# Attention, GLU and MLP on one core: decode order of the first group, the place of the short block's split, one decode pace, and the order of output steps in two MLP pairs

## The chip, the core and the metric

The kernel runs on one NeuronCore of a Trainium2 chip. TensorE (PE) multiplies; VectorE (DVE), ScalarE (ACT) and GpSimd (POOL) do the element work; SyncE (SP) issues the transfers. The metric is the device time of one execution in microseconds (us); lower is better.

## The reference

Three stages run one after the other on 2304 tokens of width 512.

```python
# 1: linear attention with random features, per batch and head
h = x @ omega.T - sum(x*x)/2;  phi = exp(h - max(h)) / sqrt(m)
num = phi(q) @ (phi(k).T @ v);  x = num / (phi(q) @ sum(phi(k)) + 1e-6)
# 2: RMS norm and gated unit (d_ff 1536)
xn = x / rms(x) * rms_g
x = (silu(xn @ w_gate) * (xn @ w_val)) @ w_out
# 3: MLP (d_ff 2048)
out = silu(x @ w_in) @ w2_out
```

The weights arrive in 64-bit floating point, as two 32-bit words for each number.

## The kernel before, in words

**Numbers.** Each operand of the large products is held as a high and a low half (`hi`, `lo`), and a product is three matmuls (high by high, high by low, low by high), listed in `PASS`. Tokens stand in five blocks: four of 512 and one of 256, the short block (`j` = 4). The hidden width is cut into columns of 128, numbered `f`.

**Weights.** A weight is loaded by SP into one of two raw buffers, decoded by five DVE operations (L146 to L157) and two POOL additions (L160) into an f32 tile `m`, and then split: ACT copies the high half into a slot (L412), DVE subtracts for the low half (L416). Gate and value weights are also scaled on ACT (L168).

**Units.** After the attention and the first three columns of the gated unit comes a list `groups`: units u = 0 to 8 are the gated unit's columns 3 to 11, one column each with three weights (gate `g`, value `v`, output `o`); u = 9 to 16 are pairs of MLP columns, with four weights each (two `i`, two `p`). `std` is 9: u = 9 and 10 are computed in the plain way, the others by `quad`, which works on blocks 0 and 1 together with seven half products in place of eight, and needs sums of the token blocks (`token_sums`) and of the weights (`sum12`, `sum34`). The token sums are made twice: before u = 0, and during u = 9 and 10. The second time they are five DVE additions, two to four POOL subtractions and splits of 128x1024.

**Order on each engine.** Every engine runs its instructions in the order in which the program emits them. The program emits PE work in steps, and each step tells its length; the main loop adds it to `due`. When `due` exceeds `wq.pace`, the next job of the weight queue is emitted (`tick`) and the pace is taken off. A job that needs a slot waits until one is free. While `wq.hold` is true no job is taken in this way. `need` emits jobs at once until the weight that is asked for exists. The pace is 1.6 for u = 5 to 8 (`A_PACE`) and 2.0 for the other units (`M_PACE`); before u = 0 it is 1.6.

**Output steps.** The products with `w_out` are cut into steps (`g2_glu`, L259: three matmuls and one DVE addition into `ya`, L270; in the last gated unit also an ACT copy, L272, and a DVE subtraction, L249, which give the MLP its input). They are handed on as the list `pend` and emitted between the projections of the next unit. In a plain pair `g1_mlp` emits a whole projection of 12 matmuls (L205) and then a number of them. The result of a projection is split by ACT and DVE (L198, L199) before its output step can start. PSUM has four banks for projections and four for output steps; an output step takes a bank again when the DVE addition of the fourth step before it has read it.

**First group.** The last token sum of blocks before u = 0 calls `end(1)`, which loads the value weight into the raw buffer that this sum has used; the gate's load goes out earlier, with `end(0)`. Then the queue's first jobs are an empty one, the decode of the value weight, the decode of the gate.

**Short block.** `glu_block` ends with the product of gate and value of the short block on DVE (L621) and its split (L198 on ACT, L199 on DVE). Behind it ACT has the first bank copies of the next `quad` (L529), on which the third of its half products waits.

Of the kernel before, what the change touches and what calls it, by code (L numbers as in the profile page):

```python
# [20 lines left out]
def kernel(  # L21
# [14 lines left out]
    nc = tc.nc  # L36
# [62 lines left out]
    def ps_tile(which, shape):  # L99
        p, tag, n = pools[which]  # L100
        return p.tile(shape, F32, tag=tag, name=tag, bufs=n)
# [88 lines left out]

    PASS = [(0, 0), (0, 1), (1, 0)]
    HALVES = [slice(0, 64), slice(64, P)]
    M_PACE, A_PACE, T_PACE = 2.0, 1.6, 1.2
    W_EARLY, GRAIN, GATE = 3, 3, 3

    def split_h(s, j):
# [110 lines left out]
            yield 0.216 * nn  # L307

    KH = KC // 2
    tok, sums, ready = {}, [], set()  # L310
    NSTD = 2
    std = next(u for u, g in enumerate(groups) if g[0] == 2)

# [54 lines left out]
    class WeightQueue:  # L368
# [28 lines left out]
        def plan(self, u):  # L397
            kind, _ = groups[u]
            (a0, a1), bs = self.keys(u)
            st = self.st  # L400
            ss = State()
            ss.t = {}
            hw = KH * P
            mf = lambda key: st[key].m.bitcast(F32)

            def dec(key, n):
                for k in range(7):
                    w_decode((0, 0, key, None), st[key], k, n)

            def split_hi(x, tl):  # L410
                v = tl.rearrange("p (a n) -> p a n", a=2)
                nc.scalar.activation(out=v[:, 0, :], in_=x, func=AF.Copy)  # L412
                return v

            def split_lo(x, v, eng=nc.vector):
                eng.tensor_tensor(out=v[:, 1, :], in0=x, in1=v[:, 0, :].bitcast(F32), op=ALU.subtract)  # L416

            def hi(key):
                if key[1] in "gv":
                    w_scale(st[key])  # L420
                st[key].t = split_hi(mf(key), self.slot(key))

            def lo(key):
                split_lo(mf(key), st[key].t)
                wt[key] = st[key].t

            def sum12():
                ss.x = pools["w"][1].tile([P, KC * P], F32, tag="ws", name="ws", bufs=1)
                m0, m1 = mf(a0), mf(a1)
                less(ss.x[:, :hw], m1[:, :hw], m1[:, hw:], ALU.add)  # L430
                less(ss.x[:, hw:], ss.x[:, :hw], m0[:, :hw])

            def sum34():
                m0, m1 = mf(a0), mf(a1)
                less(m1[:, :hw], m0[:, :hw], m1[:, :hw])
                less(m1[:, hw:], m0[:, hw:], ss.x[:, hw:])

            def shi(n):
                ss.t[n] = split_hi(ss.x if n == 0 else mf(a1), self.slot(("s", u, n)))

            def slo(n):
                split_lo(ss.x if n == 0 else mf(a1), ss.t[n], nc.vector if kind == 2 else nc.gpsimd)
                wt["s", u, n] = ss.t[n]

            load = self.load
            if kind == 1:
                jobs = [
                    *[(0,)] * (u == 0),
                    (0, lambda: dec(a1, 1), lambda: load(u + 1, 1, 1)),
                    *self.tail,  # L450
                    (0, lambda: dec(a0, 0), lambda: load(u, bs[0], 0)),
                    (1, lambda: hi(a1)),
                    (0, lambda: lo(a1)),
                    (1, lambda: hi(a0)),
                    (0, lambda: lo(a0), sum12),
                    (0, sum34),
                    (1, lambda: shi(0)),
                    (0, lambda: slo(0), lambda: dec(bs[0], 0), lambda: load(u + 1, 0, 0)),
                    (1, lambda: shi(1)),
                    (0, lambda: slo(1)),  # L460
                ]
                self.tail = [(1, lambda: hi(bs[0])), (0, lambda: lo(bs[0]))]
            elif std <= u < std + NSTD:
                jobs = [
                    (0, lambda: dec(a1, 1), lambda: load(u, bs[1], 1)),
                    *self.tail,
                    (0, lambda: dec(a0, 0), lambda: load(u, bs[0], 0)),
                    (1, lambda: hi(a1)),
                    (0, lambda: lo(a1)),
                    (0, lambda: dec(bs[1], 1), lambda: load(u + 1, 1, 1)),  # L470
                    (1, lambda: hi(a0)),
                    (0, lambda: lo(a0)),
                    (0, lambda: dec(bs[0], 0), lambda: load(u + 1, 0, 0)),
                    (1, lambda: hi(bs[1])),
                    (0, lambda: lo(bs[1])),
                    (0,),
                    (1, lambda: hi(bs[0])),
                    (0, lambda: lo(bs[0])),
                ]
                self.tail = []  # L480
            else:
                jobs = [
                    (0, lambda: dec(a0, 0)),
                    (0, lambda: dec(a1, 1), lambda: load(u, bs[0], 0)),
                    (1, lambda: hi(a0), lambda: load(u, bs[1], 1)),
                    (1, lambda: lo(a0), lambda: hi(a1)),
                    (0, lambda: lo(a1), sum12),
                    (0, sum34),
                    (1, lambda: shi(0)),
                    (0, lambda: slo(0)),  # L490
                    (1, lambda: shi(1), lambda: dec(bs[0], 0)),
                    (0, lambda: slo(1), lambda: load(u + 1, 0, 0)),
                    (1, lambda: hi(bs[0]), lambda: dec(bs[1], 1)),
                    (0, lambda: lo(bs[0]), lambda: load(u + 1, 1, 1)),
                    (1, lambda: hi(bs[1])),
                    (0, lambda: lo(bs[1])),
                ]
            self.jobs += [(n, fns) for n, *fns in jobs]
# [25 lines left out]
    def quad(u, ys, hs):  # L524
# [9 lines left out]
        def more(n=1):  # L534
            return [v for v in [next(ys, None) for _ in range(n)] if v is not None]
# [23 lines left out]
        yield step  # L559
        product(w1, 0, half(0, 0), pa, True)  # L560
        copy(pb, pa)
        yield from more()
        wq.need(("s", u, 0))
        s12 = wt["s", u, 0]
# [46 lines left out]
    def glu_block(f, j, hs, ys, n):  # L611
        full = blocks[j] == TB * P
        cuts = [(0, 6), (6, 12)] if full else [(0, 12)]
        for nm in "gv":
            w = wt[1, nm, f]
            p = ps_tile("ps_g" if full else "ps_y", [P, blocks[j]])
            for n0, n1 in cuts:
                yield (n1 - n0) * blocks[j] / 2365
                part(w, j, p, n0, n1)
                if nm == "v" and n1 == 12:  # L620
                    nc.vector.tensor_tensor(out=s, in0=s, in1=p, op=ALU.mult)  # L621
                elif n1 == 12:
                    s = pools["s"][0].tile([P, blocks[j]], F32, tag="s", name="s", bufs=pools["s"][1])
                    nc.scalar.activation(out=s, in_=p, func=AF.Silu)
                for _ in range(n[nm]):
                    c = next(ys, None)
                    if c is not None:
                        yield c
        hs[f] = split_h(s, j)

    def take(ys, n):
        for _ in range(n):
            c = next(ys, None)
            if c is not None:
                yield c
# [5 lines left out]
    def stream():  # L641
# [25 lines left out]
        for u, (kind, fs) in enumerate(groups):  # L667
            first, last = kind == 2 and fs[0] == 0, u == len(groups) - 1
            done = u + 1 == std
            wq.pace = A_PACE if std - 4 <= u < std else M_PACE  # L670
            hs = {j: {} for j in range(NB)}
            if std <= u < std + NSTD:
                out_of = lambda j: g2_mlp(fs, j, hs[j], first, False, False)
                ys = iter(pend)
                wq.hold = first
                yield from g1_mlp(fs[0], 0, hs[0], (), take(ys, 4))
                yield from g1_mlp(fs[1], 0, hs[0], (), take(ys, 4))
                yield from g1_mlp(fs[0], 1, hs[1], (), ys)
                wq.release(*wq.keys(u - 1)[1])
                yield from g1_mlp(fs[1], 1, hs[1], (), out_of(0))  # L680
                wq.hold = False
                if first:
                    now, later = token_sums(
                        lambda k: w_tile(1, 7, F32) if k == 2 else wq.slot(("t", k), F32),
                        lambda n: wq.release(("t", 1 - n)),
                    )
                    sums.extend(now)
                if u == std + NSTD - 1:
                    sums.extend(later)
                yield from g1_mlp(fs[0], 2, hs[2], (), out_of(1))  # L690
                yield from g1_mlp(fs[1], 2, hs[2], (), ())
            else:
                yield from quad(u, iter(pend), hs)
# [840 lines left out]
```

## Time and profile before

| | |
|---|---|
| median of 3 runs | 975.37 us (974.75 to 975.85) |
| the profiled execution | 974.8 us |
| its span, first to last instruction | 972.9 us |
| mean granted TensorE clock | 0.995 |
| PE busy | 949.4 us, 98% of the span |
| DVE busy | 698.6 us, 72% |
| ACT, POOL busy | 431.5 us, 416.7 us |

1.9 us lie outside the span. Times within the trace count from its start. In a row of the timeline stand the start, the length from the first start to the last end of the merged instructions, the engine, the line, the operation, what it writes and reads, the shape and the count; in brackets the idle time of the engine just before and what ended it. The end of a matmul is modelled, so distances are taken from start to start.

### The profile page before, as it was taken

How to read it: one execution, taken by the hardware profiler on the slowest of the kernel's cores; microseconds unless marked ns; L12 is line 12 of the kernel's file. 1: busy time of each engine (PE TensorE's matmuls, PEld its weight loads, DVE VectorE, ACT ScalarE, POOL GpSimd, SP SyncE). 2: the span in 40 equal slices, each digit the busy share in tenths (PEclk: the TensorE clock that was granted, in tenths of full speed). 3: DMA queues.
4: the chain of work that ended last, by engine and by line, in shares of the span. 5: the costliest groups of instructions: out<-in, count | busy, mean ns of one | idle time of the engine just before them, and what ended most of it. 6: DMA issues, size and time to landing. Idle time of an engine off the chain costs nothing. (4 is left out here: it accounts for less than half of the span.)

```text
span 972.9 us, 17023 instructions
## 1 busy us (share of the span) xinstructions
PE 949.4 (98%) x6570; PEld 793.6 (82%) x6570; DVE 698.6 (72%) x1368; ACT 431.5 (44%) x978; POOL 416.7 (43%) x402
## 2 busy tenths in 40 slices
PE   8999999997999999999999989999999999999998
PEld 6888878886888888887887867887888888888887
DVE  6998989646677677777779796467675666666643
ACT  6999786533324324323332335534333333333321
POOL 8888745305445335336436231442333343424200
PEclk9999999998999999999999999999999999999999
DMA  8655543011111111111122120011011111111023
GB/s 192 167 135 132 144 126 96 1 44 44 47 62 44 44 44 44 44 44 43 44 65 66 44 66 1 22 44 44 25 63 35 53 44 43 44 44 44 1 76 120
DMA packets 79490, 60.42 MB, mean 62 GB/s; under 512 B 27313, under 2 KB 73649, under 8 KB 79409
## 3 DMA queue, kind: packets, MB, share of 16 engines
q1 hardware_dynamic: 79136, 59.26, 21.3%
q8 instruction: 52, 0.85, 0.4%
q14 instruction: 30, 0.24, 0.1%
q10 hardware_dynamic: 272, 0.07, 0.0%
HBM read 49.87 MB, written 4.72 MB: 56 GB/s over the span
## 5 line engine op out<-in xcount | busy, mean ns | idle before, releaser
L160 POOL TENSOR_TENSOR m<-m,raw 128x512 int32<-128x512 int32 x136 | 208.2, 1533 | 332.4 <-DVE m L157 169.4
L205 PE MATMUL g<-xs,w 128*128 128x512 f32 x1056 | 255.5, 390 | 0.0
L205 PEld LDWEIGHTS g<-xs,w 128*128 128x128 f32 x1056 | 197.7, 188 | 40.8
L292 PE MATMUL y<-w,h 128*128 128x512 f32 (+1 forms) x870 | 206.6, 388 | 1.5 <-DVE h L199 1.3
L292 PEld LDWEIGHTS y<-w,h 128*128 128x128 f32 x870 | 162.3, 188 | 35.8 <-DVE h L199 1.8
L259 PE MATMUL y<-h,w 128*128 128x512 f32 (+1 forms) x648 | 159.4, 373 | 9.6 <-ACT h L198 5.7
L199 DVE TENSOR_TENSOR h<-s,h 128x512 fp32r<-128x512 f32 (+1 forms) x134 | 101.1, 760 | 74.9 <-ACT h L198 74.1
L259 PEld LDWEIGHTS y<-h,w 128*128 128x128 f32 x648 | 114.8, 191 | 33.0 <-ACT h L198 6.1
L270 DVE TENSOR_TENSOR ya<-y,ya 128x512 f32<-128x512 f32 (+1 forms) x200 | 123.4, 632 | 25.5 <-PE y L259 25.4
L303 DVE TENSOR_TENSOR ya<-y,ya 128x512 f32<-128x512 f32 (+1 forms) x127 | 84.8, 681 | 62.9 <-PE y L292 62.3
L198 ACT ACTIVATE h<-s 128x512 fp32r<-128x512 f32 (+1 forms) x134 | 77.0, 585 | 118.6 <-DVE s L621 60.7
L518 PE MATMUL g<-xs,w 128*128 128x512 f32 x360 | 91.7, 390 | 0.0
L412 ACT ACTIVATE w<-m 128x512 fp32r<-128x512 f32 x74 | 46.6, 629 | 90.7 <-POOL m L160 67.9
L416 DVE TENSOR_TENSOR w<-m,w 128x512 fp32r<-128x512 f32 x65 | 60.4, 930 | 29.6 <-ACT w L412 29.3
L1051 ACT ACTIVATE e<-b,nb 128x128 f32<-128x128 f32 x272 | 75.9, 424 | 7.7 <-issue 4.3
L518 PEld LDWEIGHTS g<-xs,w 128*128 128x128 f32 x360 | 67.1, 188 | 13.9
L518 PE MATMUL g<-w,w 128*128 128x512 f32 x270 | 69.1, 391 | 1.9 <-ACT g L529 1.9
L205 PEld LDWEIGHTS y<-xs,w 128*128 128x128 f32 x480 | 61.7, 191 | 5.3 <-DVE ya L270 3.1
L205 PE MATMUL y<-xs,w 128*128 128x256 f32 x480 | 62.6, 283 | 2.7 <-DVE ya L270 2.7
L518 PEld LDWEIGHTS g<-w,w 128*128 128x128 f32 x270 | 49.9, 188 | 12.8 <-ACT g L529 2.8
L1019 DVE TENSOR_REDUCE small<-b 128x4 f32<-128x512 f32 (+1 forms) x80 | 51.3, 642 | 6.3 <-PE b L1002 2.9
L541 ACT ACTIVATE s<-s 128x512 f32<-128x512 f32 x21 | 13.3, 632 | 77.7 <-DVE s L546 77.7
(119 smaller groups left out, 1159.6 us busy)
## 6 DMA issues: line engine op xcount, KB each, us to landing
raw<-in_moe_w_out_dram SPq DMA_DIRECT2D x28, 512.0 KB, 3.6
raw<-in_moe_w_in_dram SPq DMA_DIRECT2D x16, 512.0 KB, 3.6
raw<-in_moe_w_gate_dram SPq DMA_DIRECT2D x12, 512.0 KB, 3.6
raw<-in_moe_w_val_dram SPq DMA_DIRECT2D x12, 512.0 KB, 3.6
qT<-e SPq DMA_DIRECT2D x72, 64.0 KB, 2.6
x<-in_k_dram SPq DMA_DIRECT2D x16, 256.0 KB, 3.8
x<-in_q_dram SPq DMA_DIRECT2D x16, 256.0 KB, 3.4
va<-in_v_dram SPq DMA_DIRECT2D x32, 128.0 KB, 4.2
```

The source lines that it names most:

```text
L160: tt(out=mi, in0=mi, in1=(low if step == 5 else high).bitcast(I32), op=ALU.add)
L198: nc.scalar.activation(out=ht[:, 0, :], in_=s, func=AF.Copy)
L199: nc.vector.tensor_tensor(out=ht[:, 1, :], in0=s, in1=ht[:, 0, :].bitcast(F32), op=ALU.subtract)
L205: nc.tensor.matmul(out=ps, lhsT=w[:, a, cc * P:(cc + 1) * P], rhs=xs[j][:, c, cc, :], start=(n == 0), stop=(n == 3 * KC - 1),)
L259: nc.tensor.matmul(out=ps, lhsT=wt[1, "o", f][:, a, d * P:(d + 1) * P], rhs=hs[f][:, c, :], start=(n == 0), stop=(n == nn - 1),)
L270: nc.vector.tensor_tensor(out=y[:, d, :], in0=ps, in1=y[:, d, :], op=ALU.add)
L292: nc.tensor.matmul(out=ps, lhsT=hs[f][:, a, t * P:(t + 1) * P], rhs=wt[2, "p", f][:, c, d0:d1], start=(n == 0), stop=(n == nn - 1),)
L303: nc.vector.tensor_tensor(out=o[:, t, d0:d1], in0=ps, in1=o[:, t, d0:d1], op=ALU.add)
L416: eng.tensor_tensor(out=v[:, 1, :], in0=x, in1=v[:, 0, :].bitcast(F32), op=ALU.subtract)
L518: nc.tensor.matmul(out=ps, lhsT=w[:, a, (c0 + c) * P:(c0 + c + 1) * P], rhs=x(b, c), start=(start and n == 0), stop=(n == 3 * KH - 1), ski ...
L1019: nc.vector.tensor_reduce(out=st.mx.rearrange("p (j e) -> p e j", e=2)[:, e], in_=st.ps[e], axis=AX.X, op=ALU.max)
L1051: nc.scalar.activation(out=st.e[r][:, :, h, :] if blocks4 else st.e[r][:, h, :], in_=src.rearrange("p (a f) -> p a f", a=4) if blocks4 els ...
```

## The change

In `plan`, the first group (u = 0) has a job list of its own: the gate is decoded first, then comes the empty job, then the value weight, and the splits follow in the same order. The raw buffers are refilled in that order too. The pace is 1.8 for all units below `std`, and before them. At the end of the jobs of u = 9 a job stands that can't be taken (it asks for 1024 free slots); the program takes it off after the fourth projection of this pair, so no job of u = 10 is emitted before that. The split of the short block goes into a list `wait`, which `quad` empties after its first bank copy, or a plain pair at its start. In the two plain pairs the first four projections are cut into two halves, with output steps after each half: in u = 9 two and one for each projection (before, they stood as four, four and four behind the first three), in u = 10 two and two, then one and one, and at the fourth projection all that is left, with the steps of block 0.

```diff
-    M_PACE, A_PACE, T_PACE = 2.0, 1.6, 1.2
+    M_PACE, A_PACE, T_PACE = 2.0, 1.8, 1.2
...
-            if kind == 1:
+            if u == 0:
                 jobs = [
-                    *[(0,)] * (u == 0),
+                    (0, lambda: dec(a0, 0), lambda: load(u, bs[0], 0)),
+                    (0,),
+                    (0, lambda: dec(a1, 1), lambda: load(u + 1, 1, 1)),
+                    (1, lambda: hi(a0)),
+                    (0, lambda: lo(a0)),
+                    (1, lambda: hi(a1)),
+                    (0, lambda: lo(a1), sum12),
+                    (0, sum34),
+                    (1, lambda: shi(0)),
+                    (0, lambda: slo(0), lambda: dec(bs[0], 0), lambda: load(u + 1, 0, 0)),
+                    (1, lambda: shi(1)),
+                    (0, lambda: slo(1)),
+                ]
+                self.tail = [(1, lambda: hi(bs[0])), (0, lambda: lo(bs[0]))]
+            elif kind == 1:
+                jobs = [
                     (0, lambda: dec(a1, 1), lambda: load(u + 1, 1, 1)),
                     *self.tail,
                     (0, lambda: dec(a0, 0), lambda: load(u, bs[0], 0)),
...
                 self.tail = []
+                if u == std:
+                    jobs.append((1 << 10,))
...
         copy(pb, pa)
+        while wait:
+            wait.pop(0)()
         yield from more()
...
+        if full:
+            hs[f] = split_h(s, j)
+        else:
+            wait.append(lambda: hs.update({f: split_h(s, j)}))
+
+    def mlp_block(f, j, hs, ys, n):
+        wq.need((2, "i", f))
+        p = ps_tile("ps_g", [P, blocks[j]])
+        for k in range(2):
+            yield 3 * KH * blocks[j] / 2365
+            part(wt[2, "i", f], j, p, 3 * KH * k, 3 * KH * (k + 1))
+            yield from take(ys, n[k])
+        s = pools["s"][0].tile([P, blocks[j]], F32, tag="s", name="s", bufs=pools["s"][1])
+        nc.scalar.activation(out=s, in_=p, func=AF.Silu)
         hs[f] = split_h(s, j)
...
-            wq.pace = A_PACE if std - 4 <= u < std else M_PACE
+            wq.pace = A_PACE if u < std else M_PACE
...
-                yield from g1_mlp(fs[0], 0, hs[0], (), take(ys, 4))
-                yield from g1_mlp(fs[1], 0, hs[0], (), take(ys, 4))
-                yield from g1_mlp(fs[0], 1, hs[1], (), ys)
-                wq.release(*wq.keys(u - 1)[1])
-                yield from g1_mlp(fs[1], 1, hs[1], (), out_of(0))
+                while wait:
+                    wait.pop(0)()
+                each = [(2, 1)] * 4 if first else [(2, 2), (1, 1), (0, 0), (0, 0)]
+                for n, k in enumerate(each):
+                    if n == 3:
+                        ys = chain_of(ys, out_of(0))
+                        wq.release(*wq.keys(u - 1)[1])
+                    yield from mlp_block(fs[n % 2], n // 2, hs[n // 2], ys, k if n < 3 else (k[0], 9))
                 wq.hold = False
                 if first:
+                    assert wq.jobs.pop(0)[0] == 1 << 10
```

## Rows read from the trace of the kernel before

**Rows 1.** The page: its first line.
```profile
span 972.9 us, 17023 instructions
```

**Rows 2.** Windows: length, busy us (instructions) of PE, PEld, DVE, ACT, POOL; clock, DMA.
```profile
220.00:230.00 10.00, 5.30 (x12) 3.90 (x13) 7.34 (x11) 4.71 (x12) 7.95 (x8) 0.68 0.35 106
460.00:470.00 10.00, 8.63 (x38) 7.14 (x39) 8.33 (x18) 4.41 (x10) 3.82 (x3) 1.00 0.35 107
560.00:570.00 10.00, 6.58 (x34) 5.46 (x33) 10.00 (x13) 2.89 (x5) 5.33 (x4) 0.92 0.33 99
```

**Rows 3.** Timeline, PE in the third gated unit: the pace of matmuls without waits.
```profile
308.94 1.58 PE L205 MATMUL y<-xs,w 128*128 128x256 f32 x12
310.35 0.86 PE L259 MATMUL y<-h,w 128*128 128x512 f32 x3
...
313.16 1.53 PE L518 MATMUL g<-xs,w 128*128 128x512 f32 x6
314.53 0.84 PE L259 MATMUL y<-h,w 128*128 128x512 f32 x3
```

**Rows 4.** Timeline of the last steps before u = 0, all engines.
```profile
203.20 0.38 SPq L136 DMA_DIRECT2D raw<-in_moe_w_gate_dram  x1
...
212.88 1.22 DVE L331 TENSOR_TENSOR xs<-raw,xs 128x1024 fp32r<-128x1024 f32 x1
...
213.44 5.60 PE L205 MATMUL g<-xs,w 128*128 128x512 f32 x24
...
217.55 0.43 DVE L146 TENSOR_SCALAR m<-raw 128x512 uint32<-128x512 uint32 x1 [2.85 <-DMA raw<-in_moe_w_val_dram]
...
219.23 0.69 DVE L270 TENSOR_TENSOR ya<-y,ya 128x512 f32<-128x512 f32 x1
219.40 2.69 POOL L160 TENSOR_TENSOR m<-m,raw 128x512 int32<-128x512 int32 x2 [18.58 <-DVE m L157]
...
220.88 1.50 DVE L149 TENSOR_SCALAR raw<-raw 128x512 uint32<-128x512 uint32 x1
...
223.31 0.68 DVE L228 TENSOR_TENSOR s<-s,g 128x512 f32<-128x512 f32 x1
...
224.70 5.79 PE L259 MATMUL y<-h,w 128*128 128x512 f32 x12 [5.66 <-ACT h L198]
...
230.28 5.74 PE L205 MATMUL g<-xs,w 128*128 128x512 f32 x24
```

**Rows 5.** Waits of PE: engine, line, releaser; us in total, times, longest.
```profile
PE y L259 <- DVE ya L270: 3.3, 4, 1.3
...
PE g L518 <- ACT g L529: 1.9, 2, 1.4
```

**Rows 6.** Timeline, ACT at the start of the quad of u = 6.
```profile
460.42 0.42 ACT L198 ACTIVATE h<-s 128x256 fp32r<-128x256 f32 x1 [5.07 <-DVE s L621]
```

**Rows 7.** Timeline from the last gated unit to block 0's output in u = 9.
```profile
557.60 0.42 DVE L146 TENSOR_SCALAR m<-raw 128x512 uint32<-128x512 uint32 x1
...
562.50 1.58 PE L205 MATMUL y<-xs,w 128*128 128x256 f32 x12
...
564.66 3.14 DVE L249 TENSOR_TENSOR xs<-ya,xs 128x512 fp32r<-128x512 f32 x2
...
568.46 2.93 PE L205 MATMUL y<-xs,w 128*128 128x256 f32 x12 [2.71 <-DVE ya L270]
...
570.72 0.42 DVE L146 TENSOR_SCALAR m<-raw 128x512 uint32<-128x512 uint32 x1
...
593.83 5.69 PE L292 MATMUL y<-w,h 128*128 128x512 f32 x24 [0.18 <-DVE ya L270]
```

**Rows 8.** One window, from block 2 of u = 9 to u = 10; columns as in group 2.
```profile
599.35:623.94 24.59, 24.59 (x121) 20.85 (x120) 12.17 (x15) 12.64 (x22) 10.98 (x5) 1.00 0.07 22
```

**Rows 9.** Timeline, plain pairs: two splits, and PE's wait for one.
```profile
609.50 2.92 DVE L199 TENSOR_TENSOR h<-s,h 128x512 fp32r<-128x512 f32 x2 [1.77 <-ACT h L198]
...
664.69 3.47 PE L292 MATMUL y<-w,h 128*128 128x512 f32 x14 [1.32 <-DVE h L199]
```

More of the change, by code (lines that the diff above doesn't have):

```diff
@@ L309 @@
     KH = KC // 2
-    tok, sums, ready = {}, [], set()
+    tok, sums, ready, wait = {}, [], set(), []
     NSTD = 2
```

## The prediction

> **What bounds the kernel now.** I read the page first, then PE's clock and load in windows of 10 us, then the list of PE's waits, and last the timeline of all engines around each place where PE waits. PE bounds the kernel: its matmuls fill nearly the whole span [rows 1], and where nothing holds it back a matmul of 512 columns follows the one before it after (314.53 - 313.16)/6 = 0.228 us, one of 256 columns after (310.35 - 308.94)/12 = 0.1175 us [rows 3]. So the change can only win back time in which PE stands still or runs at the lower clock. There is little of it and it lies in a few places, so I price place by place: matmuls counted in the code between two rows, times these two durations, against the distance of the rows.
>
> Before u = 0: 213.44 to 230.28 holds 24 + 12 = 36 matmuls of 512, 8.2 us of work in 16.84 us; lost 8.6 [rows 4]. 5.66 of this is one wait. After it the granted clock is at the lower of its two levels, 1.2 GHz, for most of the window (mean 0.68) [rows 2], and 12 matmuls take 230.28 - 224.70 = 5.58 where 2.74 would do: 2.84 more [rows 4].
>
> At the starts of quads: two waits for a bank copy (L529), 1.9 together [rows 5].
>
> At the end of u = 7: of the four waits of an output step for a `ya` addition the longest, 1.3 [rows 5]; the other three lie in the next place.
>
> From the short block of u = 8 to block 0's output in u = 9: 562.50 to 593.83 is 31.33 us and holds 78 matmuls of 512 and 36 of 256, 17.8 + 4.2 = 22.0 us; lost 9.3 [rows 7]. A part is clock: the window of 560 shows 0.92 [rows 2].
>
> In u = 10: one wait of 1.3 for a split [rows 9].
>
> Together 22.4 us, out of 974.8 us for the profiled execution. All steps below are sums against this 974.8; the median of the runs shown, 975.37, is 0.6 above it.
>
> **The first group's order.** Here the chain is: the value weight's raw buffer comes free with the last token sum (L331, 212.88 + 1.22), its load lands at 217.55, DVE stands before its decode for 2.85 us, then decodes it, adds a `ya`, and decodes the gate as well; only then comes the product of gate and value of block 0 (L228, 223.31) [rows 4]. PE's output steps wait for the split of this product. The gate's words were loaded at 203.20, so its decode needs no transfer. With the change it starts where L331 ends, about 214.1; five operations last 219.23 - 217.55 = 1.68, so it ends about 215.8, its two POOL additions (2.69) about 218.6, and the two `ya` additions fit before 217.55. The value's decode then starts between 217.55, if POOL does not hold it up, and 218.6, if it does; L149 beside a POOL addition took 1.50 where L146 took 0.43 [rows 4], so I take 218.6. Then L228 starts at 218.6 + 1.68 = 220.3 and not at 223.31: 3.0 won (4.1 at the other end). PE's wait shrinks from 5.66 to about 2.6 (1.6). The same number of jobs, transfers and splits is issued; the refill of the value's raw buffer, for u = 1, moves one job back, a whole unit ahead of its use. If the clock stays up after the shorter wait, 2.84 are won too, less about 0.5 for the second output matmul, which still waits for the low half: 2.3. Sum 5.3.
>
> **The short block's split.** The bank copies of the quad stand behind L198 on ACT, which waited 5.07 us for the DVE product L621 [rows 6]. With the change the first copy needs only its own matmuls. What is late next is the copy `e`, which now stands behind the split and is read three half products later, and the split itself, read by the last four output steps of the quad. I take the whole 1.9; the other end is 0, if PE then meets `ya` additions that are just as late.
>
> **The even pace.** In `glu_block` a half projection and an output step add 1.30 + 0.65 = 1.95 to `due`. A pace of 1.6 leaves 0.35 over each time, so that from u = 5 a second job falls into the same step every fifth time or so; 1.8 leaves 0.15, and in u = 0 to 4, where 2.0 took less than one job for each step, it is just above one. The weight decodes are not fewer, but in u = 7 the output weight's decode and the POOL split behind it come one or two steps (1.3 to 2.0 us) earlier, and the MLP decodes behind them are no longer pushed together. I take 1.0 of the 1.3 (ends 0 and 1.3). What u = 0 to 4 pay is put at nothing: no wait of [rows 5] lies there, and DVE has room; if that cover is gone, a wait as in u = 7 is the price, 1.3.
>
> **The stop in the queue and the spread steps.** By 557.60 all four weights of u = 9 have been decoded; the decodes from 557.60 to 570.72 are three (557.60, 561.27, 570.72), all for u = 10 [rows 7]. They fall where DVE has two operations for each output step, because the last unit also splits `xs`; two of these subtractions took 3.14 beside POOL's additions, and PE then waited 2.71 [rows 7]. With the stop these three decodes leave the stretch: 3 x 1.68 on DVE, 3 x 2.69 on POOL [rows 4], and two low splits of 0.69. Then the first projections of u = 9: with four steps behind a projection DVE needs 4 x 2 x 0.69 + 0.69 = 6.2 us while PE needs 24 x 0.228 = 5.5; with three steps it is 4.8 against 21 x 0.228 = 4.8. So DVE no longer falls behind, but gains nothing either: the short block's product and split, which now stand there, are not hidden, about 0.8 (two operations of 256 columns, ACT's took 0.42 [rows 6]), and I leave one more wait of 0.5. Won 8.0 of 9.3. The low end is the stall in front of 568.46 alone: 568.46 - 562.50 less 12 x 0.1175 and 3 x 0.228, 3.9. The cut of a projection in two halves itself costs nothing, since the number of matmuls and of loads of weights stays.
>
> **What the moved decodes cost.** The three decodes now come behind the fourth projection of u = 9, beside the second token sums. There DVE and POOL are busy 12.17 and 10.98 of 24.59 us, and PE waits nowhere [rows 8]. The decodes add 3 x (1.68 + 2.69) + 1.4 = 14.5, so 37.6 us of DVE and POOL work, of which most reads SBUF on both engines, stand against 24.59. They can run side by side only in part: two splits took 2.92 instead of 1.4 [rows 9]. I expect that splits come late twice in the plain pairs, at 1.3 each, the wait at 664.69 being the nearest row: 2.6 lost. Ends: 0, and 8 (the rival below). The wait at 664.69 itself I leave as it is.
>
> **Sum.** 5.3 + 1.9 + 1.0 + 8.0 - 2.6 = 13.6; 974.8 - 13.6 = 961.2, and 961.8 with the 0.6 of the median.
>
> **Rivals.** (1) The clock falls again at the shortened wait before u = 0. A wait of 2.71 was followed by a lower clock, the window that holds one of 1.4 shows 1.00 [rows 2, 5, 7]; 2.6 lies by the first, but the stretch in front of the 2.71 was itself broken by waits, and here PE works without a gap before. Price 2.3: 964.1.
>
> (2) The moved decodes and the token sums shut each other out. If no DVE and POOL operation overlaps there, 13 us of the 37.6 do not fit into the stretch, and late splits are passed on into u = 10, where PE waits more often; I put 8 in place of 2.6, that is six waits of 1.3: 967.2. For it speaks L149's 1.50, against it that the list of waits shows PE almost never waiting for a split. The Trainium skill, in "SBUF — State Buffer", section "Who interferes with whom", says that DVE operations with two SBUF inputs, or in the modes that use both ports, and GpSimd operations that read SBUF exclude one another for a whole instruction. By that rule this rival's count is the right one and the sum would be 967.2; L149's 1.50 agrees with it.
>
> (3) The even pace doesn't help: the backlog on DVE before u = 9 comes from the `xs` splits alone. Then the pace gives 0 and only 3.9 of 9.3 come back: 1.0 + 4.1 more, 966.9. Against it: the decodes stand in the very rows of the stall.
>
> (4) Slower: the two input weights of u = 10 are not ready when it starts. Between the stop and 623.94 lie 24.59 us, in which steps for about eleven jobs are emitted; the low split of the second weight is the seventh. It decides when fewer than seven are taken; then `need` emits them in line, each 1.68 + 2.69 + 2 x 0.69 = 5.8 us of waiting, with 2.84 for the clock as behind 5.66. Two of these are 17.2 against 13.6 + 2.6 = 16.2 won elsewhere: 1.0 over the time before, 976.4.
>
> (5) The change doesn't do what it says: the waits pass to the next late operation, and the time stays at 975.
>
> **Chances.** The forecast 0.42, the clock 0.30, the crowded pair 0.14, no help from the pace 0.08, slower 0.03, no change 0.03. A difference of 0.2% is about what a measurement of this kernel can tell from none. Faster by more: 0.94; within: 0.03; slower: 0.03. The range reaches down to 957.5 (all of 9.3, the other end of the decode's start) and up to 967.5, which takes in cases 1 to 3.
>
> **What would show it.** Right: before u = 0 DVE writes the gate's decode behind L331 with no wait for a transfer, and PE's wait there is 1.6 to 2.7 with the clock above 0.9 in that window; no wait of L518 for L529; three decodes fewer between the last gated unit's second block and u = 9; fewer than 2 us lost over the 78 and 36 matmuls; new waits for L199 or `h` between block 2 of u = 9 and the end of u = 10, of 1 to 3 us. Wrong: PE's wait before u = 0 over 4 us, a clock near 0.7 there, or waits for splits in the plain pairs of more than 5 us together.

## The result and the profile after

The changed kernel took 964.98 us in the median of 4 runs (964.62 to 965.69), the kernel before 975.42 us beside it (974.75 to 975.85). The ratio is 0.9894, 95% interval 0.9877 to 0.9912: faster by 10.4 us. The forecast was 961.8, so the sign and the range held, and the likeliest value lay 3.2 us too low. The profiled execution took 964.6 us, 10.2 less than that of before.

Both kernels issue 6570 matmuls, and at the ends of the stretches below the n-th is the same one in every kernel, so distances between two of them can be set side by side. Such a distance is longer than the work of its matmuls (0.228 us each for 512 columns) by what PE loses in it, to waits or to the lower clock. Behind the start, five stretches differ by more than 0.2 us, and all the rest together by 0.03:

| stretch, from start to start | before | after | won | forecast |
|---|---|---|---|---|
| start of the trace to the last projection before u = 0 | 213.44 | 215.12 | -1.7 | 0 |
| A: that projection and the outputs behind it, 36 matmuls | 16.85 | 12.99 | 3.9 | 5.3 |
| Q: from 443 us (before) to the short block of u = 8, 560 | 119.65 | 115.51 | 4.1 | 1.9 + 1.0 |
| S: from there to block 2 of u = 9, 138 | 36.85 | 28.63 | 8.2 | 8.0 |
| U: outputs of u = 9, at 598.40 after, 24 | 5.44 | 10.98 | -5.5 | -2.6 |
| W: in u = 10, 40 | 10.70 | 9.41 | 1.3 | 0 |

The sum is 10.3. U, where the change loses, is the main miss of the forecast. The first line of the page, beside [rows 1]:

```profile
span 962.7 us, 17025 instructions
```

PE's list of waits, beside [rows 5]:

```profile
PE y L292 <- DVE h L199: 3.3, 1, 3.3
PE y L259 <- ACT h L198: 2.5, 1, 2.5
PE kv L1119 <- DMA vat<-in_v_dram: 1.8, 1, 1.8
...
PE y L292 <- DVE ya L270: 0.8, 1, 0.8
```

The waits for bank copies and all four for a `ya` addition at L259 are gone from it. Two long ones stand at the top: the known one before u = 0, shorter, and a new one for a split. The windows that hold these two show the lower clock, the one that held the stall at the end of u = 8 does not any more (columns as in [rows 2]):

```profile
220.00:230.00 10.00, 7.31 (x25) 5.30 (x24) 7.11 (x13) 4.72 (x12) 5.02 (x6) 0.83 0.31 107
560.00:570.00 10.00, 10.00 (x45) 8.26 (x45) 8.00 (x15) 4.71 (x9) 0.00 (x0) 1.00 0.01 2
600.00:610.00 10.00, 6.68 (x24) 5.19 (x23) 9.85 (x14) 3.35 (x7) 4.56 (x3) 0.83 0.29 99
```

Stretch A in the timeline, beside [rows 4]:

```profile
215.12 5.60 PE L205 MATMUL g<-xs,w 128*128 128x512 f32 x24
215.70 0.42 DVE L146 TENSOR_SCALAR m<-raw 128x512 uint32<-128x512 uint32 x1
...
217.54 2.70 POOL L160 TENSOR_TENSOR m<-m,raw 128x512 int32<-128x512 int32 x2 [15.06 <-DVE m L157]
...
219.36 1.17 DVE L146 TENSOR_SCALAR m<-raw 128x512 uint32<-128x512 uint32 x1 [0.70 <-DMA raw<-in_moe_w_val_dram]
...
221.79 0.67 DVE L228 TENSOR_TENSOR s<-s,g 128x512 f32<-128x512 f32 x1
...
223.18 0.49 PE L259 MATMUL y<-h,w 128*128 128x512 f32 x1 [2.46 <-ACT h L198]
...
223.91 4.37 PE L259 MATMUL y<-h,w 128*128 128x512 f32 x11 [0.23 <-DVE h L199]
...
228.11 5.62 PE L205 MATMUL g<-xs,w 128*128 128x512 f32 x24
```

The gate's decode starts at 215.70 and waits for no transfer. The value's L146 ends at 220.53, just behind POOL's additions (220.24). The product L228 stands behind all of it. Eleven matmuls then take 228.11 - 223.91 = 4.20 where 2.51 would do.

Stretch S, PE and two rows of DVE, beside [rows 7]: its first 114 matmuls, up to 578.10, now take 22.03, which is their work; one wait is left behind them.

```profile
556.08 1.58 PE L205 MATMUL y<-xs,w 128*128 128x256 f32 x12
...
578.10 1.55 PE L292 MATMUL y<-w,h 128*128 128x512 f32 x6
...
579.40 0.69 DVE L199 TENSOR_TENSOR h<-s,h 128x512 fp32r<-128x512 f32 x1 [1.64 <-ACT h L198]
580.01 0.42 DVE L270 TENSOR_TENSOR ya<-y,ya 128x256 f32<-128x256 f32 x1
...
580.49 4.38 PE L292 MATMUL y<-w,h 128*128 128x512 f32 x18 [0.83 <-DVE ya L270]
```

The wait is for a `ya` addition that stands on DVE behind the split of the fourth projection.

Stretch U, where before no wait stood [rows 8]:

```profile
590.33 8.20 POOL L160 TENSOR_TENSOR m<-m,raw 128x512 int32<-128x512 int32 x4 [41.50 <-ACT ya L301]
...
591.79 1.22 DVE L345 TENSOR_TENSOR w<-xs 128x1024 f32<-128x1024 f32 x1
...
598.40 1.88 PE L292 MATMUL y<-w,h 128*128 128x512 f32 x5
598.50 2.82 POOL L319 TENSOR_TENSOR w<-w,w 128x1024 f32<-128x1024 f32 x1
...
599.14 2.46 DVE L146 TENSOR_SCALAR m<-raw 128x512 uint32<-128x512 uint32 x1
...
602.87 2.38 DVE L199 TENSOR_TENSOR h<-s,h 128x512 fp32r<-128x512 f32 x2
...
603.60 5.94 PE L292 MATMUL y<-w,h 128*128 128x512 f32 x19 [3.32 <-DVE h L199]
...
609.38 2.88 PE L205 MATMUL g<-xs,w 128*128 128x512 f32 x12
```

Five matmuls (1.14 us of work) take 603.60 - 598.40 = 5.20: 4.1 lost waiting. The next 19 take 5.78 in place of 4.33: 1.4 lost to the clock. On DVE a decode of u = 10 stands in front of the two splits, and its first operation, which took 0.42 at 215.70, lasts 2.46 while POOL's token-sum subtraction runs.

### The profile page after: what moved, and what is told of

Read it like the earlier page. It is cut to its first block, busy times and chain, and to the rows that moved or that the text cites. A ratio compares the mean times of both kernels' runs of the same rounds, so it can differ in the third digit from the quotient of the medians.

```text
span 962.7 us, 17025 instructions
## 1 busy us (share of the span) xinstructions
PE 947.6 (98%) x6570; PEld 793.8 (82%) x6570; DVE 709.2 (74%) x1368; ACT 432.8 (45%) x978; POOL 415.3 (43%) x402
## 4 chain that ended last, share of the span: by engine, by line
PE 90%; DVE 4%; ACT 2%; DMA 1%; POOL 1%; SPq 1%; issue 1%; DVEq 0%; POOLq 0%
PE g L205 22%; PE y L292 20%; PE g L535 15%; PE y L259 13%; PE y L205 6%; PE b L1039 3%; PE b L205 2%; PE b L1439 2%; PE kv L1119 2%; PE b L1012 2%; PE b L1223 2%; PE b L1199 1%; PE b L1319 1%; POOL m L160 1%; DVE h L199 1%
## 5 line engine op out<-in xcount | busy, mean ns | idle before, releaser
L160 POOL TENSOR_TENSOR m<-m,raw 128x512 int32<-128x512 int32 x136 | 204.1, 1503 | 323.7 <-issue 176.9
L292 PE MATMUL y<-w,h 128*128 128x512 f32 (+1 forms) x870 | 209.4, 390 | 4.2 <-DVE h L199 3.3
L259 PE MATMUL y<-h,w 128*128 128x512 f32 (+1 forms) x648 | 157.4, 369 | 2.7 <-ACT h L198 2.5
L199 DVE TENSOR_TENSOR h<-s,h 128x512 fp32r<-128x512 f32 (+1 forms) x134 | 108.4, 815 | 65.5 <-ACT h L198 64.2
L259 PEld LDWEIGHTS y<-h,w 128*128 128x128 f32 x648 | 114.4, 190 | 24.0 <-ACT h L198 2.9
L535 PE MATMUL g<-xs,w 128*128 128x512 f32 x360 | 91.7, 390 | 0.0
L416 DVE TENSOR_TENSOR w<-m,w 128x512 fp32r<-128x512 f32 x65 | 65.7, 1012 | 27.5 <-ACT w L412 27.5
L535 PEld LDWEIGHTS g<-xs,w 128*128 128x128 f32 x360 | 67.1, 188 | 13.9
L535 PE MATMUL g<-w,w 128*128 128x512 f32 x270 | 68.8, 390 | 0.0
L535 PEld LDWEIGHTS g<-w,w 128*128 128x128 f32 x270 | 50.1, 188 | 10.0
```

What stands on the lines that cost most here:

```text
L160: tt(out=mi, in0=mi, in1=(low if step == 5 else high).bitcast(I32), op=ALU.add)
L199: nc.vector.tensor_tensor(out=ht[:, 1, :], in0=s, in1=ht[:, 0, :].bitcast(F32), op=ALU.subtract)
L259: nc.tensor.matmul(out=ps, lhsT=wt[1, "o", f][:, a, d * P:(d + 1) * P], rhs=hs[f][:, c, :], start=(n == 0), stop=(n == nn - 1),)
L292: nc.tensor.matmul(out=ps, lhsT=hs[f][:, a, t * P:(t + 1) * P], rhs=wt[2, "p", f][:, c, d0:d1], start=(n == 0), stop=(n == nn - 1),)
L535: nc.tensor.matmul(out=ps, lhsT=w[:, a, (c0 + c) * P:(c0 + c + 1) * P], rhs=x(b, c), start=(start and n == 0), stop=(n == 3 * KH - 1), ski ...
```

## The experiments

Twelve kernels ran, with the kernel before beside them at 974.78 (1 to 4), 975.24 (6 to 9) and 975.13 (median of 9 runs; 5 and 10 to 12). 1 to 9 were timed once, 10 to 12 in 4, 4 and 5 runs. The start ahead of u = 0, where no instruction is edited, took from 212.00 to 215.45 in the profiles, so a single time can't tell 2 us. The stretches behind it repeat within 0.2 where nothing was changed in them, but for A and U with a fallen clock (within 0.5 and 1.1), and the verdicts go by these distances. In us:

| kernel | time | A | Q | S | U | W |
|---|---|---|---|---|---|---|
| before | 974.8 | 16.85 | 119.65 | 36.85 | 5.44 | 10.70 |
| changed | 964.6 | 12.99 | 115.51 | 28.63 | 10.98 | 9.41 |
| 1 order alone | 970.15 | 11.41 | 119.66 | 36.90 | 5.44 | 10.72 |
| 2 no stop | 964.08 | 12.67 | 115.51 | 36.59 | 5.44 | 9.47 |
| 3 old pace | 963.32 | 12.99 | 117.04 | 28.61 | 11.26 | 9.42 |
| 4 split at once | 965.09 | 13.00 | 115.51 | 28.61 | 11.17 | 9.47 |
| 5 old pace, split at once | 968.91 | 12.79 | 119.65 | 28.66 | 11.99 | 9.43 |
| 6 steps as before | 964.86 | 12.99 | 115.51 | 27.81 | 11.28 | 10.69 |
| 7 value later | 959.08 | 8.36 | 115.51 | 28.63 | 11.05 | 9.45 |
| 8 stop behind one job | 960.24 | 13.01 | 115.51 | 31.27 | 5.44 | 9.43 |
| 9 no subtractions | 959.95 | 12.57 | 115.51 | 28.62 | 7.57 | 9.40 |
| 10 both | 955.63 | 8.36 | 115.51 | 31.27 | 5.44 | 9.43 |
| 11 both, steps as before | 955.53 | 8.36 | 115.51 | 29.88 | 5.44 | 10.71 |
| 12 both, more steps | 955.34 | 8.35 | 115.51 | 29.93 | 5.44 | 9.40 |

**1. The first group's order alone**: the kernel before, with the changed kernel's job list for u = 0 and nothing else.

```diff
+            if u == 0:
+                jobs = [
+                    (0, lambda: dec(a0, 0), lambda: load(u, bs[0], 0)),
...
-                    *[(0,)] * (u == 0),
```

> The kernel before with the first group's order alone. Theory: the product of gate and value of block 0 comes 1.5 to 3 us earlier, PE's wait before u = 0 shrinks from 5.7 to about 2.5, and the clock still falls behind it, as in the changed kernel: 3.8 us are won in that place and nothing elsewhere, 971.6. Rival: the order alone does nothing there, because the queue's pace (1.8 in place of 1.6) is what moved the jobs: the wait stays at 5.7 and the time at 975.4.

A fell by 5.4, the other four stretches stayed. So the order does it, and the rival fell. The wait is the same 2.46, but the clock, which the theory expected to fall behind it, did not. PE's timeline:

```profile
222.03 0.50 PE L259 MATMUL y<-h,w 128*128 128x512 f32 x1 [2.46 <-ACT h L198]
222.75 2.79 PE L259 MATMUL y<-h,w 128*128 128x512 f32 x11 [0.22 <-DVE h L199]
...
225.38 5.60 PE L205 MATMUL g<-xs,w 128*128 128x512 f32 x24
```

Eleven matmuls take 2.63 (4.20 in the changed kernel), the window from 220 to 230 shows 1.00 and not 0.83. So the order is worth 5.4 with the clock up and 3.9 with it down. Of the nine kernels with a wait of 2.4 to 2.5 here only this one kept the clock: in the changed kernel and seven others (2 to 6, 8, 9) it fell, and A is 12.57 to 13.01.

**2. Without the stop.**

```diff
-                if u == std:
-                    jobs.append((1 << 10,))
...
-                    assert wq.jobs.pop(0)[0] == 1 << 10
```

> The changed kernel without the stop in the queue. Theory: the stop is what takes the three decodes out of the last gated unit, and what puts them beside the token sums. Without it the wait of 3.3 us for a split in u = 9 and the lower clock behind it go (5.7 less), and between the short block of u = 8 and block 0's output in u = 9 some 4 to 9 us are lost again: 963 to 968. Rival: the pace of 1.8 has thinned out the decodes in any case; then that stretch stays as it is and the time is 959.

PE's timeline at the last gated unit shows the stall again:

```profile
553.32 1.58 PE L205 MATMUL y<-xs,w 128*128 128x256 f32 x12
...
558.03 2.34 PE L205 MATMUL y<-xs,w 128*128 128x256 f32 x12 [2.43 <-DVE ya L270]
```

S is back at 36.59, 0.3 from before, and U at 5.44. The stop is worth 8.0 in S and costs 5.5 in U, 2.4 net; the spread and the pace without it win 0.3 in S. The theory held, the rival did not.

**3 and 4. The old pace; the split at once.**

```diff
-    M_PACE, A_PACE, T_PACE = 2.0, 1.8, 1.2
+    M_PACE, A_PACE, T_PACE = 2.0, 1.6, 1.2
...
-            wq.pace = A_PACE if u < std else M_PACE
+            wq.pace = A_PACE if std - 4 <= u < std else M_PACE
```

> The changed kernel with the old paces (2.0, then 1.6 from u = 5). Theory: the pace gave the 1.6 us at the end of u = 7 and little else: the wait of 1.3 for a `ya` addition there is back, 966.6, at most 968. Rival: the pace is what emptied the last gated unit; then 9 us come back at its end, 974.

```diff
-        if full:
-            hs[f] = split_h(s, j)
-        else:
-            wait.append(lambda: hs.update({f: split_h(s, j)}))
+        hs[f] = split_h(s, j)
```

> The changed kernel with the short block's split again right behind its product. Theory: bank copies of the quads wait behind it once more, twice or so, 1.5 to 2.5 us together: 966.5 to 967.5. Rival: with the even pace DVE is no longer late at the starts of quads, so the split's place no longer matters: 965.0, no wait for L529.

Without the pace (3) Q is 1.5 longer, by one wait at the end of u = 7, and S does not move: the stop empties S without the pace. That holds by stretch; the time of 963.32 lies below that of the changed kernel because the start of this trace is 3.1 us shorter. In PE's list of waits:

```profile
PE y L259 <- DVE ya L270: 1.2, 1, 1.2
```

Without the later split (4) nothing changes, as the rival said. Neither kernel has a wait for a bank copy.

**5. Both of these undone.** The edits of 3 and 4 together.

> The changed kernel without the even pace and without the short block's moved split, so the new order, the stop and the spread alone. Each of these two alone left no wait for a bank copy (L529). Theory: the two are redundant, each removes the same late product in front of the copy, so with both gone the waits come back: about 2 us for L529 at the starts of quads, and the 1.2 at the end of u = 7, 3 to 3.5 us lost by place. Rival: the new order of the first group removed them, since it changes which job falls into which step from u = 0 on: no wait for L529, and only the 1.2 at the end of u = 7.

In PE's list of waits both kinds are back (L535 and L546 are L518 and L529 of before):

```profile
PE g L535 <- ACT g L546: 1.9, 2, 1.4
...
PE y L259 <- DVE ya L270: 1.3, 1, 1.3
```

Q is back at 119.65, that of before: the theory held, with 4.1 lost and not 3 to 3.5. So of the 4.1 in Q the split alone wins 2.6 (119.65 to 117.04), the pace alone 4.1, both together 4.1: beside the even pace the split's new place is worth nothing.

**6. The output steps as before**, with the stop kept.

```diff
-                each = [(2, 1)] * 4 if first else [(2, 2), (1, 1), (0, 0), (0, 0)]
...
+                yield from g1_mlp(fs[0], 0, hs[0], (), take(ys, 4))
+                yield from g1_mlp(fs[1], 0, hs[0], (), take(ys, 4))
```

> The changed kernel with the output steps of the two plain pairs again behind whole projections (four, four, four). Theory of the prediction: DVE needs 6.2 us for four steps and a split where PE needs 5.5, so some 2 us and waits for PSUM banks come back in the first projections of u = 9: 967. Rival: the stop alone has freed DVE, and the four banks even out the rest; then the wait of 0.8 for a `ya` addition in the fourth projection goes as well, 964.

PE's list of waits, and its timeline at the outputs of block 0 in u = 9:

```profile
PE y L292 <- DVE h L199: 4.6, 2, 3.3
```

```profile
577.54 5.69 PE L292 MATMUL y<-w,h 128*128 128x512 f32 x24
```

S is 0.8 shorter, and W has its wait of 1.3 back (the second of the two in the list). The rival was right about S: the first 114 matmuls take 22.28, only 0.25 more than with the spread, and the 24 behind them 5.53 and not 6.60. The spread loses in u = 9 and wins in u = 10; 0.5 is left of it.

**7. The value's decode one step later**, by a second empty job ahead of it.

```diff
                     (0,),
+                    (0,),
                     (0, lambda: dec(a1, 1), lambda: load(u + 1, 1, 1)),
```

> The changed kernel with one more empty job ahead of the value weight's decode in u = 0, which puts this decode behind the product of gate and value of block 0 on DVE. Theory: what PE still waits for before u = 0 (2.5 us) is only this decode, with the transfer that it waits for. The wait falls under 0.5, the clock stays up there: 2.5 + 2.3 less, 960. Rival: the next late operation takes its place (the value weight's split, or the weights' sums that the first quad needs), and PE waits about as long in front of or in u = 0: 964 to 965.

The timeline before u = 0:

```profile
217.53 0.68 DVE L228 TENSOR_TENSOR s<-s,g 128x512 f32<-128x512 f32 x1
...
219.51 3.08 PE L259 MATMUL y<-h,w 128*128 128x512 f32 x12
219.67 0.41 DVE L146 TENSOR_SCALAR m<-raw 128x512 uint32<-128x512 uint32 x1
```

The product L228 now goes ahead of the decode, PE does not wait, and A is 8.36, its work: 4.6 less than in the changed kernel. No later stretch pays, so the theory held.

**8. The stop one job further back**, so that the first decode of u = 10 is let through ahead of u = 9.

```diff
-                if u == std:
-                    jobs.append((1 << 10,))
+                if u == std + 1:
+                    jobs.insert(1, (1 << 10,))
```

> The changed kernel with the stop one job later, so that one of the three decodes runs in the last gated unit and two beside the token sums. Theory: the wait in u = 9 comes from the decodes' crowding; with one fewer it shrinks under 1.5 us and the clock stays up, while the last gated unit has room for one decode: 3 to 5 less, 960 to 962. Rival: already one decode in the last gated unit brings the stall of 2.6 us at its end back, as with no stop: 965 to 967.

The timeline, the decode that was let through and U's outputs:

```profile
551.46 0.42 DVE L146 TENSOR_SCALAR m<-raw 128x512 uint32<-128x512 uint32 x1
...
599.43 5.60 PE L292 MATMUL y<-w,h 128*128 128x512 f32 x24
```

One decode has moved to 551.46, U is 5.44 without a wait, and S is 2.6 longer: 2.9 won. The theory held for U. The rival was half right: no single stall of 2.6 came back, but several waits for `ya` of at most 0.9 cost S as much.

**9. Without the four POOL subtractions of the second token sums.** This leaves out a part of the computation: the sums of token blocks (four DVE additions, L345 in the changed kernel) are used without being subtracted from one another.

```diff
-    def token_sums(temp, end):
+    def token_sums(temp, end, sub=True):
+        minus = less if sub else (lambda *a: None)
...
-            lambda: less(u[0], u[1], u[0]),
+            lambda: minus(u[0], u[1], u[0]),
...
                         lambda n: wq.release(("t", 1 - n)),
+                        False,
```

> The changed kernel without the four POOL subtractions of the second token sums, so the sums that go into the products of u = 11 and later are not those of the reference. Theory: POOL and DVE shut each other out; in the changed kernel the third decode's first operation took 2.46 us beside such a subtraction and held up the split that PE waits for. Without the subtractions this operation takes 0.4, the wait of 3.3 falls to about 1.2 and the clock stays up: 4.4 less, 960.5. Rival: it is the decode's own five operations ahead of the split that count; the wait stays near 3 and the time at 964 to 965.

The timeline of U, DVE and PE:

```profile
597.96 0.43 DVE L146 TENSOR_SCALAR m<-raw 128x512 uint32<-128x512 uint32 x1
...
599.65 2.40 DVE L199 TENSOR_TENSOR h<-s,h 128x512 fp32r<-128x512 f32 x2
...
600.39 4.60 PE L292 MATMUL y<-w,h 128*128 128x512 f32 x19 [1.25 <-DVE h L199]
```

The decode stands in the same place on DVE, but its first operation takes 0.43 in place of 2.46. PE's wait shrinks by the same 2.0, from 3.32 to 1.25, and the clock holds: U is 7.57. The theory held.

**10 to 12. Both improvements (7 and 8) together; the same with the output steps of before; the same with four, four and four steps behind the first three half-cut projections of u = 9 alone.**

```diff
-                each = [(2, 1)] * 4 if first else [(2, 2), (1, 1), (0, 0), (0, 0)]
+                each = [(2, 2), (2, 2), (3, 1), (0, 0)] if first else [(2, 2), (1, 1), (0, 0), (0, 0)]
```

> The changed kernel with two edits together: before u = 0 the value weight's decode is taken one output step later, and the stop stands behind the first job of u = 10. If the two places are independent, their gains by place add: 5.6 us before u = 0 (no wait for the high half, clock 1.00 there) and 4.5 us from the end of u = 8 to the end of u = 9, so 964.8 - 10.1 = 954.7, and 954 to 957 with what the profiles differ by in the attention. Rival: the gain in one place is given back further on, since the decodes of u = 0 or u = 10 are only pushed on: 958 or more, with new waits between u = 0 and u = 7 or in u = 10.

> As the run with both edits, and with the output steps of the two MLP pairs as before the change (four behind each of the first two projections). With the stop behind one job, DVE's queue in the first projections of u = 9 is short of output steps, not of time: the waits for ya there (0.7 to 0.9 each, about 1.5 together more than in the changed kernel) should shrink, but the wait of 1.3 in u = 10 returns. If both hold: within 1 us of the run with both edits. If the spread is what keeps u = 9 fed: 2 us slower.

> As the run with both edits, with four output steps behind each of the first two projections of u = 9 again, but u = 10's steps left spread as the change has them. It should have the better half of each: the waits for ya at the first projections of u = 9 smaller and no wait of 1.3 in u = 10: 1 to 1.5 us below the run with both edits. Rival: the waits for ya are set by the decode that the stop let through and not by how the steps are laid out: no difference.

Against the kernel before: 0.9797 (0.9784 to 0.9810), 0.9797 (0.9784 to 0.9811) and 0.9788 (0.9771 to 0.9804). PE's list of waits of the third holds, behind the attention, only these:

```profile
PE y L259 <- DVE ya L270: 0.8, 1, 0.8
PE y L205 <- DVE ya L270: 0.8, 1, 0.8
```

Both stand in S. The gains of 7 and 8 add, as expected. All three beat the median of the changed kernel by 9.4 to 9.6 us, of which A gives 4.6 and S with U 2.9 to 4.3; in the profiles the start adds 0.8 to 2.0. By stretch the third is 1.3 better than either other, at the end of S against the first and in W against the second; the medians can't show it. Where its expectation put the gain it did not come: the first 114 matmuls of S take 24.49 in the first and in the third alike.

## Why the prediction was right or wrong

**The first group's order (5.3, measured 3.9).** The mechanism and the times were right (203.20 in [rows 4] is when the gate's load is issued, not when it has landed, but its decode did not wait for it): set off by the 1.7 by which this trace starts later, L228 was due at 222.0 and came at 221.79, the wait was to be 2.6 and was 2.46. The failed step is the clock, which was put at staying up. Rival 1 took place, at a price of 1.6 (12.99 - 11.41, with the same wait on both sides) where the text had 2.3. That PE works without a gap ahead of the wait was the reason given for the higher clock; experiment 1 went that way, the changed kernel and seven others did not, with the same work ahead of it. What decides between them stays open.

**The short block's split (1.9) and the even pace (1.0): measured 4.1 together.** Both places were right, the split of the gain was not: the pace alone does all of it, also at the bank copies, where it was priced at nothing. The price of 1.9 was only the waits; the stretch gave 2.6 there.

**The stop and the spread steps (8.0, measured 8.2).** The size was right. The first 114 matmuls lost nothing, so all 9.3 came back; neither the uncovered product (0.8) nor the wait left open (0.5) showed there. The 1.1 lost in the 24 behind them is another cost: the spread puts three steps into the fourth projection, right ahead of the outputs of block 0. Without steps in that projection these 24 take 5.53 and 5.44 (experiments 6 and 12), with them 6.60 and 6.78 (the changed kernel and experiment 10). So the step that credited the spread is wrong: by its sum four steps put DVE behind by 0.7 for each projection (6.2 against 5.5), but with the stop in place that cost 0.25 in all, and the spread makes S longer by 0.8. Rival 3 fell: all 9.3 came back where it had 3.9, and the pace is worth 1.5 in Q.

**The moved decodes (-2.6, measured -5.5).** The failed term. The place and the kind, late splits in the plain pairs, were right. The size was taken from the one wait of 1.3 of [rows 9]. But the late split is not one operation late: a whole decode stands in front of it, stretched by POOL, and the long wait brings the clock down as well. Experiment 8 shows that it is the crowding of three decodes: with two there U has no wait. Rival 2's mechanism is shown by experiment 9, where L146 is short without the subtraction. In the changed kernel it starts at 599.14, 0.64 behind POOL's subtraction, and ends at 601.60, 0.28 behind the end of it. The Trainium skill, in "SBUF — State Buffer", section "Who interferes with whom", says that between GpSimd and a DVE operation in a mode that uses both ports, whoever issues first holds the shared pair of ports for the whole instruction and the other blocks. The trace agrees, with 2.46 beside the subtraction and 0.43 without it; it does not tell the mode of L146. Rival 2's form, six waits spread into u = 10, was wrong: it is one place, and u = 10 has none.

**What was put at nothing.** The wait of [rows 9] in u = 10 went with the spread there (experiment 6): 1.3 more. The start of the trace was 1.7 later; there PE waits 1.8 for a transfer of `in_v`, which no other of the profiles lists. The change does not reach that far; how much of the difference of the medians such a start explains can't be told from times alone.

Together: 1.4 (clock) + 2.9 (decodes) + 1.7 (start) more time than forecast, 1.2 (Q) + 0.2 (S) + 1.3 (u = 10) less; that is 3.3 of the 3.4 between 961.2 and the profiled 964.6. That the time came out so near is in part luck: 6.0 us of misses one way, 2.7 the other. The low end of the range, 957.5, was not covered by its two reasons, which give 961.8 - 1.3 - 1.1 = 959.4. Rival 4 did not come about: u = 10 shows no wait for a weight. Rival 5 fell with the time. Of the signs named ahead, the gate's decode, PE's wait, the bank copies, the three decodes and the work of S came as said; the clock before u = 0 (0.83, not above 0.9) and the size of the wait for a split (3.3, not at most 3) did not.

## What to carry to other kernels

Moving background work out of a stall is worth what it wins there less what it costs where it lands: price the landing by the whole group of instructions that comes to stand in front of the next urgent one, each as long as it is beside the other engine's work, and then by the clock behind the wait. Before each of two edits is credited with a gain, undo each alone and then both: here one covered the other. Where one urgent operation is late behind a decode, try first to let it pass; one empty job gave more than a third of what the whole change had won.

## What the runs showed of the hardware

The same wait of 2.46 us behind the same 24 matmuls was followed by the higher clock in one kernel and by the lower in others (11 matmuls in 2.63 and 4.20 us). Behind 1.25 us in stretch U it stayed up (1.00 from 600 to 610 in experiment 9, where the changed kernel shows 0.83 behind 3.32). In the attention, too, waits of one length went both ways: behind the wait of 1.8 for `in_v` the changed kernel shows a granted clock of 0.50 from 132.0 to 135.4, and experiment 6 shows 1.00 from 110 to 120, with another wait of 1.8 at 111.33.

POOL is also held up by DVE. Of its four additions that begin at 590.33, which took 8.20 us together, the first took 3.84, while DVE ran a decode and a 128x1024 sum one behind the other until 593.01, none of them longer than elsewhere; in stretch A two additions took 2.70.
